# Delta rule and MLP mixer on one core: every step of the recurrence as 64x64 products on compact state, with another order of issue

## The chip, the cores and the metric

The kernel runs on one NeuronCore of one Trainium2 chip. The metric is the device time of one execution in microseconds, the median of several runs. The engines named below are TensorE (PE, with its weight loads as PEld), VectorE (DVE), ScalarE (ACT), GpSimd (POOL) and the queue that issues the DMAs (SP).

## The reference

Two blocks follow each other, all in float32. The first is a delta rule, a recurrence over 768 positions for each of 4 batch elements and 8 heads with 48 features:

```
k_n = k / (norm(k) + 1e-6)
state = 0                                    # (B, H, 48, 48)
for t in range(768):
    y[t]  = q[t] @ state
    v_old = state @ k_n[t]
    state = state + beta[t] * outer(k_n[t], v[t] - v_old)
```

Its output, with the heads side by side, is x of shape (4, 768, 384). The second block is an MLP mixer:

```
u   = x + transpose(relu(transpose(x) @ w_tok1) @ w_tok2)     # along the 768 positions, 256 wide
out = u + relu(u @ w_ch1) @ w_ch2                             # along the 384 channels, 1536 wide
```

## The kernel before

**The recurrence in blocks.** The 768 positions of a batch element are cut into 12 chunks of 64 (C = 64), so there are 48 steps r0 to r47, and r12, r24 and r36 begin a new batch element with an empty state. Within a chunk the recurrence is solved with a 64x64 triangular matrix. `prep` builds the matrices of two chunks from k and q (a unit u), `invert` inverts the triangular blocks of 32 by rows on DVE, `join` puts the two halves together with 32x32 products, and the result lies in the tile `gm`. A step then is a short chain: the state is multiplied with k (and q), v is subtracted, the result is multiplied with the inverse, and that product `w` makes the update of the state and the rest of the output `y`.

**Two forms of a step.** The first element (r0 to r11) runs through `recur_early`. It holds the state of each of the 8 heads once, as 48 rows in one half of the partitions, and makes five groups of 8 products (head by head, 64 rows and 64 columns of the array, 48 columns of moving data): `p_k` (L655), the first part of `p_y` (L665), `p_w` (L676), `p_s` (L684) and the second part of `p_y` (L695). The eight products of a group alternate between two quarters of the array, one in each half of the rows and of the columns. The other three elements (r12 to r47) run through `recur`. It holds two heads at a time as a block-diagonal state twice as wide (`s_bd`, `rw_bd`), half of it zeros, and makes three groups of 4 products of the whole array with 96 columns of moving data: `p_q` (L730) for k and q together, `p_w` (L746) and `p_s` (L756) for state update and output together. Because the halves lie in different places, DVE subtracts in two instructions each (L734, L764) and adds the output in one or two more (L773, L776); ACT copies `w` in two (L749) and `p_q`'s q half in one (L751).

**The mixer.** `mixer(b)` takes the finished element: products `p_1` along the positions (L887) into `p_h` (L900), a transpose, then for pairs of chunks the wide products into 1536 channels (plain at L973 for the first element, a form with seven products in place of eight at L818 for the others) and back (L992). Its weights come in pieces that ACT, DVE and POOL round on their way (`round_weights`, L246 to L266).

**The order of the work.** Nothing is scheduled at run time. Every job is a generator, and a long text called `order` says which job issues its next piece: `r` is a step of the recurrence, `m` the mixer, `p`, `i`, `f`, `h`, `j`, `k`, `v` preparation and inversion, `w` a piece of weights, `s` sums of weights. `x`, `z` and `Y` are products of zeros into `p_warm` (L200, L210), which nobody reads. Each engine works through its own instructions in that order, waiting on semaphores where an operand isn't there. The PSUM pools are `prep` (2 buffers), `seq` (2), `mlp` (3) and one for `p_warm`; before, `p_y` of the early steps takes one of `mlp`, and `p_q`, `p_k`, `p_w` and `p_s` take those of `seq`.

Of the kernel before, what the change touches and what calls it, by code (L numbers as in the profile page):

```python
# [8 lines left out]
FP32 = mybir.dt.float32  # L9
# [14 lines left out]
def kernel(  # L24
# [128 lines left out]
    GW = 2 * C + D  # L153
# [6 lines left out]
    r_bd = w_bd = const.tile([128, NP, 2 * D], FP32, name="rw_bd")  # L160
    s_bd = tiles("s_bd", [128, NP, 2 * D], 2)
# [29 lines left out]
    def place(u):  # L191
        return NV + u if u < 2 else (u - 2) % NV

# [123 lines left out]
    walked = set()  # L317

# [52 lines left out]
    def gm_of(u):  # L371
        return gms[place(u)]

    def prep(u):
# [46 lines left out]
        for p in range(NP):  # L421
            nc.tensor.transpose(p_t[:, p], qp[:, 2 * p : 2 * p + 2], ident)
        turned.add((False, u))
        yield
        nc.scalar.copy(kqt_q, p_t)
        yield
        scaler.tensor_tensor(
            out=blocks(gm)[:, :, :, 2 * C :], in0=kst,
# [12 lines left out]
        for cc in range(2):  # L441
            nc.vector.tensor_tensor(  # L442
                out=blocks(gm)[:, :, cc, 0 : 2 * C].rearrange(
                    "s p (two n) -> s p two n", two=2
                ),
                in0=p_g[cc],
                in1=mb[:, :, cc, None, :].to_broadcast([128, NP, 2, C]), op=ALU.mult,
            )
            yield
# [32 lines left out]
    def quarters(u):  # L482


        rnd, j = round_of[u]
        for i in range(4):
            r = slice(HB * i, HB * i + HB)
            cols = slice(HB * (i % 2), HB * (i % 2) + HB)
            lo = (4 * j + i) * NB
            yield (  # L490
                gm_of(u)[r, :, cols], (r, slice(0, HB), slice(j * NB, j * NB + NB)),
                slice(lo, lo + NB),
            )
# [114 lines left out]
    def join(u):  # L608

        done = joined_16 if u < NCH else inverted  # L610
        wt = gm_of(u)[:, :, 0:C]
# [23 lines left out]
    def recur_early(t):  # L635

        u, cc = divmod(t, 2)
        assert t == len(steps)  # L640
        steps.append(t)
        gm, kqt = gm_of(u), kqts[place(u)]
        if t == 0:
            xbs[0] = mlp_pool.tile([128, NCH, DM], FP32, name="xb", tag="xb")
        y = xbs[0][C * cc : C * cc + C, u].rearrange("s (p n) -> s p n", p=NP)
        s0, s1 = s_bd[t % 2][:, :, 0:D], s_bd[(t + 1) % 2][:, :, 0:D]
        w = w_bd[:, :, D : 2 * D]
        by_head = [(p, i, PAR[i ^ cc]) for p in range(NP) for i in range(2)]

        p_y = ps_mlp([128, NP, D], "p_y")  # L650
        if t > 0:
            p_k = ps_seq([128, NP, D], "p_k")
            for p, i, r in by_head:
                f = FEATS[i]
                nc.tensor.matmul(p_k[r, p], kqt[f, 2 * p + cc, 0], s0[f, p])  # L655
            yield
            assert u in scaled
            rest = r_bd[:, :, 0:D]
            nc.vector.tensor_tensor(
                out=rest, in0=p_k, in1=vsts[u][:, :, cc], op=ALU.subtract  # L660
            )
            yield
            for p, i, r in by_head:
                f = FEATS[i]
                nc.tensor.matmul(  # L665
                    p_y[r, p], kqt[f, 2 * p + cc, 1], s0[f, p],
                    start=(p == 0), stop=False,
                )
            yield

        assert u in scaled and u in joined
        if t == 0:
            rest = vsts[u][:, :, cc]
        p_w = ps_seq([128, NP, D], "p_w")
        for p, i, r in by_head:
            nc.tensor.matmul(p_w[r, p], gm[r, 2 * p + cc, 0:C], rest[r, p])  # L676
        yield
        nc.scalar.copy(w, p_w)
        yield

        if t < NQ - 1:
            p_s = ps_seq([128, NP, D], "p_s")
            for p, i, r in by_head:
                nc.tensor.matmul(p_s[FEATS[i], p], gm[r, 2 * p + cc, 2 * C :], w[r, p])  # L684
            yield
            for f in FEATS:
                if t > 0:
                    nc.vector.tensor_tensor(
                        out=s1[f], in0=s0[f], in1=p_s[f], op=ALU.subtract
                    )  # L690
                else:
                    nc.vector.tensor_copy(out=s1[f], in_=p_s[f])
            yield
        for p, i, r in by_head:
            nc.tensor.matmul(  # L695
                p_y[r, p], gm[r, 2 * p + cc, C : 2 * C], w[r, p],
                start=(t == 0 and p == 0), stop=(p == NP - 1),
            )
        if cc == 1:
            walked.add(u)  # L700
        yield
        for i in range(2):
            nc.scalar.mul(
                y[:, :, D * i : D * i + D], p_y[PAR[i ^ cc]], 1.0 if t else -1.0
            )
        written.add(t)
        if t == NQ - 1:
            for t_ in (w_bd, *s_bd):
                nc.gpsimd.memset(t_, 0.0)
        yield  # L710

    def recur(t):

# [9 lines left out]
        s0, s1 = s_bd[t % 2], s_bd[(t + 1) % 2]  # L723
        lo, hi = PAR
        ends = (slice(0, D), slice(D, 2 * D))

        if c > 0:
            p_q = ps_seq([128, NP, 2 * D], "p_q")
            for p in range(NP):
                nc.tensor.matmul(p_q[:, p], kqt[:, 2 * p + cc], s0[:, p])  # L730
            yield
            for i in range(2):
                r = PAR[i ^ cc]
                nc.vector.tensor_tensor(  # L734
                    out=r_bd[r, :, ends[i ^ cc]], in0=p_q[lo, :, ends[i]],
                    in1=vsts[u][r, :, cc], op=ALU.subtract,
                )
        else:
            for r, e in zip(PAR, ends):
                nc.gpsimd.tensor_copy(out=r_bd[r, :, e], in_=vsts[u][r, :, cc])  # L740
        yield

        assert u in scaled and u in joined
        p_w = ps_seq([128, NP, 2 * D], "p_w")
        for p in range(NP):
            nc.tensor.matmul(p_w[0 : C + 1, p], gm[:, 2 * p + cc, 0 : C + 1], r_bd[:, p])  # L746
        yield
        for r, e in zip(PAR, ends):
            nc.scalar.copy(w_bd[r, :, e], p_w[lo, :, e])  # L749
        if c > 0:  # L750
            nc.scalar.copy(y, p_q[hi])  # L751
        yield

        p_s = ps_seq([128, NP, 2 * D], "p_s")
        for p in range(NP):
            nc.tensor.matmul(p_s[0 : C + D, p], gm[:, 2 * p + cc, C:], w_bd[:, p])  # L756
# [3 lines left out]
        if c < NQ - 1:  # L760
            for i, e in enumerate(ends):
                f, e2 = FEATS[i], ends[i ^ cc]
                if c > 0:
                    nc.vector.tensor_tensor(  # L764
                        out=s1[f, :, e], in0=s0[f, :, e], in1=p_s[C : C + D, :, e2],
                        op=ALU.subtract,
                    )
                else:
                    nc.vector.tensor_copy(out=s1[f, :, e], in_=p_s[C : C + D, :, e2])
        if c == 0:  # L770
            nc.scalar.mul(y, p_s[lo], -1.0)
        elif cc == 0:
            nc.vector.tensor_tensor(out=y, in0=y, in1=p_s[lo], op=ALU.add)  # L773
        else:
            for i, e in enumerate(ends):
                nc.vector.tensor_tensor(  # L776
                    out=y[:, :, e], in0=y[:, :, e], in1=p_s[lo, :, ends[1 - i]],
                    op=ALU.add,
                )
# [266 lines left out]
    for t in range(B * NQ):  # L1046
        jobs[f"r{t}"] = recur(t) if t >= NQ else recur_early(t)
# [17 lines left out]
    w10*5 Y x z k0 b w2 w1 x*4 Y k0*5 p0 w2*3 w1*2 k1 p0 w3 b*2 k2 k1 Y k3 p0 w2  # L1065
    p0*4 x p0*3 k1*4 p1 w3 p0*2 p1 p0 x k2*3 p1*5 k4 k2 k3 Y k4 Y k4 w3 p1*2 k4 k2
    p2 p1*2 k3 p2 v1 v0 p1 k3 p1 k3*2 p2*2 p3*2 p2*5 w3 p3*3 x Y z p0 p1 p2*4 p0 w1
    z p3*5 Y p0*2 k4 p3 k4 p4*2 p3*2 p1*2 p2 x p4 p2*3 z*2 p3*2 v0 v1 w18 p3*2 p4 p1
    p4 i0*2 k5 v0 w1 p4*2 i0*3 w3 i0*3 p4*4 k6*2 k7 i0*2 w18 i0*2 k6*2 x p4 i0*2
    k5*3 k6 k5 k7 w18 k6 k7 Y z k7*2 i0*2 v1 w6 v0 h1 p5 p4*2 w18 h0 w6 p5 w6*2 p6 z  # L1070
    i0 h0 p6 z p5 f1 h1 k8 w6 f0 w18 f0*2 v0 f0 p4 f1*3 k5 w13*2 h2 w13 f2*2 h2 h0*4
    p7 h0 x z w8*2 j0 w8 p5 h1 w13 h1*2 w13 j0*2 p5 z f2*2 h1 w8 p6 j0*2 h1 p7 p5*4
    h2 w8 w11 v1 h2 w11 r0*2 w11 h2*3 z r0 p5*2 w17*2 p6 p4*2 w17 r0 r1 w17 p5*3
    k8*2 z v1 w17 p5*3 p6 r1 h3 j1 i1 r0 w14 w11 h3 w14 r1*2 k9 k8 r1 w11 w14 i1
    j1*2 k9*3 r1*3 w0 k8 x p6*3 f3 p6 f3 p6 p7 j1*2 v2*3 i1 r2*2 z p7 i1 r2 w0 i1*2
    j2 i1 f3*2 r2*5 h3*3 i1 Y w14 h3 r0 h3 r3*2 k9 i1 j2*2 p8 k9 w0 k8 k7 i1 p8 r3
    p6 k10*2 p6*2 r1 r3 w0*2 x r3*3 v2*2 j2*2 w14 r2 k10 p7*2 j3 r4*3 r3 i1 r4 w9 j3
# [93 lines left out]
```

## Time and profile before

| | |
|---|---|
| median of 3 runs | 699.59 us (699.56 to 701.43) |
| span of the profiled execution | 693.3 us, TensorE's granted clock 0.983 on average |
| around it | the page gives the span alone, so the profiled execution's own time is not told apart from it; the median of the runs stands 6.3 us above the span |
| PE busy | 663.1 us (96%), 7904 products |
| DVE busy | 477.4 us (69%), 1263 instructions |
| ACT busy | 279.1 us (40%) |
| POOL busy | 106.0 us (15%) |

A float32 product is two records in the profile, so a group of 8 products counts as x16 and a group of 4 as x8. PE is pipelined: a product's duration holds the time from its issue to its last result, and the time that it takes from the others is read from the distance of starts or from the chain. Numbers in the views are microseconds unless marked ns.

### The profile page before, as it was taken

What the parts mean: (1) busy time and instruction counts of PE and PEld (TensorE: products, weight loads), DVE (VectorE), ACT (ScalarE), POOL (GpSimd) and SP (SyncE); (2) the same over time, 40 slices, a digit from 0 to 9 for tenths busy, and PEclk for the clock granted to TensorE, in tenths of its full rate; (3) what the DMA queues carried; (4) which work ended last, traced back from release to release, by engine and by line L of the source; (5) the groups of instructions that cost most, each with busy time, mean ns of one, the idle gap of its engine ahead of it and who ended that gap; (6) DMA issues with size and microseconds to landing.
All of it is one profiled execution on the core that took longest, in us unless ns stands there. A gap on an engine that the chain in (4) does not pass through costs nothing.

```text
span 693.3 us, 19064 instructions
## 1 busy us (share of the span) xinstructions
PE 663.1 (96%) x7904; PEld 589.5 (85%) x7904; DVE 477.4 (69%) x1263; ACT 279.1 (40%) x659; POOL 106.0 (15%) x130
## 2 busy tenths in 40 slices
PE   8759989899999999999999999999999999999998
PEld 6437766558999998978999999978999997999997
DVE  7999997998889854797676886368854532252433
ACT  7647674436542243123652515124425240132230
POOL 3236254133322021001120101101000000000000
PEclk9959999999999999999999999999999999999999
DMA  9755667544343244214443103110030000000000
GB/s 180 129 134 109 142 141 173 131 114 97 76 106 73 57 81 78 60 40 93 80 76 75 32 22 78 33 35 16 4 74 2 1 24 1 23 2 24 0 25 23
DMA packets 146902, 46.17 MB, mean 67 GB/s; under 512 B 138080, under 2 KB 141280, under 8 KB 146816
## 3 DMA queue, kind: packets, MB, share of 16 engines
q1 hardware_dynamic: 146816, 44.95, 30.1%
q8 instruction: 62, 1.02, 0.6%
q14 instruction: 24, 0.20, 0.1%
HBM read 35.49 MB, written 9.44 MB: 65 GB/s over the span
## 4 chain that ended last, share of the span: by engine, by line
PE 85%; ACT 4%; DVE 4%; DMA 3%; issue 2%; POOL 1%; SPq 0%; ACTq 0%; POOLq 0%; DVEq 0%
PE p_o L992 24%; PE p_r L818 7%; PE p_c L818 7%; PE p_c L973 6%; PE p_d L818 5%; PE p L887 5%; PE p_h L900 5%; PE p_q L730 4%; PE p_s L756 4%; PE p_w L746 4%; PE p_g L436 3%; PE p_warm L200 3%; DMA d<-in_moe_w_ch_dram 2%; PE p_z L619 2%; PE p_x L628 1%
## 5 line engine op out<-in xcount | busy, mean ns | idle before, releaser
L992 PE MATMUL p_o<-wc,r 128*128 128x192 f32 x720 | 126.4, 328 | 0.6 <-ACT u_t L914 0.6
L992 PEld LDWEIGHTS p_o<-wc,r 128*128 128x128 f32 x720 | 116.7, 190 | 2.7 <-ACT u_t L914 1.1
L918 DVE TENSOR_TENSOR xb<-xb,p_o 128x192 f32<-128x192 f32 x84 | 29.5, 351 | 61.1 <-PE p_o L992 60.8
L558 DVE TENSOR_TENSOR x<-x,sub 128x84 f32<-128x84 f32 (+24 forms) x178 | 61.0, 343 | 6.1
L553 DVE TENSOR_TENSOR sub<-x 128x84 f32<-128x84 f32 (+24 forms) x178 | 57.4, 323 | 3.8
L973 PE MATMUL p_c<-u_t,wc 128*128 128x256 f32 x216 | 50.2, 383 | 0.0
L992 PE MATMUL p_o<-wc,s 128*128 128x192 f32 x288 | 50.1, 327 | 0.0
L264 POOL TENSOR_TENSOR w_f<-w_f,d 128x384 uint32<-128x384 uint32 (+1 forms) x34 | 34.0, 1004 | 89.5 <-DVE w_f L257 45.7
L835 DVE TENSOR_TENSOR r<-p_r,r 128x384 f32<-128x384 f32 x36 | 19.9, 552 | 39.3 <-ACT r L864 29.9
L992 PEld LDWEIGHTS p_o<-wc,s 128*128 128x128 f32 x288 | 46.8, 190 | 0.0
L838 ACT ACTIVATE r<-r 128x384 f32<-128x384 f32 x72 | 37.6, 524 | 19.9 <-DVE r L835 17.5
L818 PE MATMUL p_r<-u_t,wc 128*128 128x128 f32 x324 | 45.4, 276 | 0.0
L818 PE MATMUL p_c<-u_t,wc 128*128 128x128 f32 x324 | 45.4, 276 | 0.0
L358 POOL TENSOR_TENSOR v_st<-v_st,nrm 128x384 f32<-128x384 f32 x24 | 20.4, 851 | 162.3 <-DMA v_st<-in_v_dram 112.1
L973 PEld LDWEIGHTS p_c<-u_t,wc 128*128 128x128 f32 x216 | 39.7, 190 | 5.3 <-issue 0.5
L415 POOL TENSOR_TENSOR mb<-mask_c,cs 128x512 f32<-128x512 f32 x20 | 21.2, 1060 | 143.2 <-DVE cs L397 137.2
L749 ACT COPY rw_bd<-p_w 64x192 f32<-64x192 f32 x72 | 22.3, 310 | 48.3 <-PE p_w L746 47.1
L818 PEld LDWEIGHTS p_r<-u_t,wc 128*128 128x128 f32 x324 | 40.7, 192 | 0.4 <-issue 0.3
L818 PEld LDWEIGHTS p_c<-u_t,wc 128*128 128x128 f32 x324 | 40.5, 192 | 0.2 <-issue 0.2
L442 DVE TENSOR_TENSOR gm<-p_g,mb 128x512 f32<-128x512 f32 x44 | 28.9, 683 | 12.5 <-PE p_g L436 12.2
L845 ACT COPY r<-p_c 128x384 f32<-128x384 f32 x18 | 8.6, 478 | 67.8 <-PE p_c L818 55.2
L200 PE MATMUL p_warm<-warm 128*128 128x512 f32 (+1 forms) x76 | 34.6, 569 | 0.4 <-issue 0.4
(185 smaller groups left out, 1308.9 us busy)
## 6 DMA issues: line engine op xcount, KB each, us to landing
d<-in_moe_w_ch_dram SPq DMA_DIRECT2D x24, 384.0 KB, 3.9
v_st<-in_v_dram SPq DMA_DIRECT2D x96, 48.0 KB, 2.7
out_dram<-xb SPq DMA_DIRECT2D x23, 192.0 KB, 1.8
kpad<-in_k_dram SPq DMA_DIRECT2D x18, 192.0 KB, 3.6
qpad<-in_q_dram SPq DMA_DIRECT2D x18, 192.0 KB, 3.6
kst<-in_k_dram SPq DMA_DIRECT2D x64, 48.0 KB, 2.8
n_dram<-gm SPq DMA_DIRECT2D x72, 32.0 KB, 1.9
gm<-w_dram SPq DMA_DIRECT2D x72, 32.0 KB, 2.1
```

The lines of the kernel that those rows point to most:

```text
L200: nc.tensor.matmul(p_warm[:, 0:m], zero, zero[:, None, :].to_broadcast([128, m, 128]))
L264: nc.gpsimd.tensor_tensor(out=f, in0=f, in1=lo, op=ALU.add)
L442: nc.vector.tensor_tensor(out=blocks(gm)[:, :, cc, 0 : 2 * C].rearrange("s p (two n) -> s p two n", two=2), in0=p_g[cc], in1=mb[:, :, cc, ...
L553: nc.vector.tensor_tensor(out=tmp, in0=y[:, :, 0:s, s : s + 1].to_broadcast([n, k, s, w]), in1=y[:, :, s : s + 1, s + 1 : m].to_broadcast( ...
L558: nc.vector.tensor_tensor(out=y[:, :, 0:s, s + 1 : m], in0=y[:, :, 0:s, s + 1 : m], in1=tmp, op=ALU.add,)
L818: nc.tensor.matmul(p[:, i], weight(g * n + i), b_, start=first and i == 0, stop=True, skip_group_check=True,)
L838: nc.scalar.activation(out, out, ACTF.Relu)
L887: nc.tensor.matmul(p_1[dh], piece_of(w1, c, 0)[:, dh * 128 : (dh + 1) * 128], xb[:, c], start=(c == 0), stop=(c == NCH - 1),)
L900: nc.tensor.matmul(p_h, piece_of(w2, j, c * 128)[:, c * 128 : (c + 1) * 128], r1[j], start=(j == 0), stop=(j == NDH - 1),)
L918: nc.vector.tensor_tensor(out=xb[:, c, e], in0=xb[:, c, e], in1=p, op=ALU.add)
L973: nc.tensor.matmul(p_c[:, k], piece_of(wc1, cb, f * 128)[:, f * 128 : (f + 1) * 128], u_t[:, cb], start=(cb == 0), stop=(cb == NCB - 1),)
L992: nc.tensor.matmul(p, a[:, m], wc2[:, m, j], start=(start and m == 0), stop=(m == NM - 1), skip_group_check=True,)
```

## The change

`recur_early` goes, and a new `recur` does all 48 steps in the compact form. The state `s_t`, the difference `rest` and `w_t` are 128x192 each, with nothing in them but the heads. The eight `p_k` products stay a group of their own. The first part of `p_y` and `p_w` are now issued product by product in turn, and so are `p_s` and the second part of `p_y`. `p_y` is written to the other half of the partitions than before, which puts two neighbouring products of different kind on two quarters in the same rows, and the next two on the other rows. `p_y` moves from the pool `mlp` to `seq`. The columns of `gm` change places (key part first, inverse second, masked product last) so that `p_s` can take 64 columns from column 0. DVE subtracts in one instruction of 128x192 for `rest` and one for the state; ACT copies `w` in one and writes `y` in two. Clearing the block-diagonal tiles on POOL (L709) and copying v there (L740) go. The text `order` is a new one throughout; it has 30 products into `p_warm` where there were 82.

```diff
-    GW = 2 * C + D
+    GW = D + 2 * C
+    KC, TC, GC = slice(0, D), slice(D, D + C), slice(D + C, GW)
-    r_bd = w_bd = const.tile([128, NP, 2 * D], FP32, name="rw_bd")
-    s_bd = tiles("s_bd", [128, NP, 2 * D], 2)
+    rest_t = const.tile([128, NP, D], FP32, name="rest")
+    w_t = const.tile([128, NP, D], FP32, name="w_t")
+    s_t = tiles("s_t", [128, NP, D], 2)
...
-    def recur_early(t):
...
     def recur(t):
...
-            p_q = ps_seq([128, NP, 2 * D], "p_q")
-            for p in range(NP):
-                nc.tensor.matmul(p_q[:, p], kqt[:, 2 * p + cc], s0[:, p])
-            yield
-            for i in range(2):
-                r = PAR[i ^ cc]
-                nc.vector.tensor_tensor(
-                    out=r_bd[r, :, ends[i ^ cc]], in0=p_q[lo, :, ends[i]],
-                    in1=vsts[u][r, :, cc], op=ALU.subtract,
...
+        heads = [(p, i, PAR[i ^ cc], PAR[1 - i]) for p in range(NP) for i in range(2)]
+        if c > 0:
+            p_k = ps_seq([128, NP, D], "p_k")
+            for p, i, r, _ in heads:
+                f = FEATS[i]
+                nc.tensor.matmul(p_k[r, p], kqt[f, 2 * p + cc, 0], s0[f, p])
+            yield
+            nc.vector.tensor_tensor(
+                out=rest, in0=p_k, in1=vsts[u][:, :, cc], op=ALU.subtract
+            )
+            yield
...
+        p_y = ps_seq([128, NP, D], "p_y")
+        p_w = ps_seq([128, NP, D], "p_w")
+        for p, i, r, o in heads:
+            if c > 0:
+                f = FEATS[i]
+                nc.tensor.matmul(
+                    p_y[o, p], kqt[f, 2 * p + cc, 1], s0[f, p],
+                    start=(p == 0), stop=False,
+                )
+            nc.tensor.matmul(p_w[r, p], gm[r, 2 * p + cc, TC], rest[r, p])
+        yield
+        nc.scalar.copy(w_t, p_w)
+        yield
+        on = c < NQ - 1
+        if on:
+            p_s = ps_seq([128, NP, D], "p_s")
+        for p, i, r, o in heads:
+            if on:
+                nc.tensor.matmul(p_s[PAR[i], p], gm[r, 2 * p + cc, 0:C], w_t[r, p])
+            nc.tensor.matmul(
+                p_y[o, p], gm[r, 2 * p + cc, GC], w_t[r, p],
+                start=(c == 0 and p == 0), stop=(p == NP - 1),
+            )
+        yield
+        if on:
+            if c > 0:
+                nc.vector.tensor_tensor(out=s1, in0=s0, in1=p_s, op=ALU.subtract)
+            else:
+                nc.vector.tensor_copy(out=s1, in_=p_s)
+            yield
+        for i in range(2):
+            nc.scalar.mul(
+                y[:, :, D * i : D * i + D], p_y[PAR[1 - i]], 1.0 if c else -1.0
+            )
...
-        jobs[f"r{t}"] = recur(t) if t >= NQ else recur_early(t)
+        jobs[f"r{t}"] = recur(t)
...
     order = """
...
```

## The prediction

> **What bounds the kernel now.** I read the page's shares and slices first, then the stretches, then the chain, then single groups on PE.
>
> ```profile
> PE 663.1 (96%) x7904; PEld 589.5 (85%) x7904; DVE 477.4 (69%) x1263; ACT 279.1 (40%) x659; POOL 106.0 (15%) x130
> PE   8759989899999999999999999999999999999998
> DVE  7999997998889854797676886368854532252433
> PEclk9959999999999999999999999999999999999999
> PE 85%; ACT 4%; DVE 4%; DMA 3%; issue 2%; POOL 1%; SPq 0%; ACTq 0%; POOLq 0%; DVEq 0%
> ```
>
> PE is full from the eighth slice on; DVE is full only in the first thirteen.
>
> ```profile
> 0.00:131.00 131.00, 108.37 (x2597) 80.09 (x2598) 115.59 (x316) 85.01 (x208) 50.93 (x65) 0.91 0.69 143
> 131.00:165.00 34.00, 31.18 (x300) 20.43 (x298) 30.58 (x74) 12.54 (x29) 11.61 (x15) 1.00 0.51 123
> 165.00:231.00 66.00, 65.26 (x653) 60.40 (x654) 58.67 (x168) 28.91 (x69) 14.03 (x15) 1.00 0.34 74
> 231.00:450.00 219.00, 219.00 (x2373) 204.93 (x2372) 152.67 (x408) 79.45 (x191) 25.90 (x31) 1.00 0.31 64
> 450.00:694.00 244.00, 239.29 (x1986) 223.69 (x1985) 119.87 (x301) 73.21 (x164) 3.52 (x4) 1.00 0.07 18
> ```
>
> The columns behind the length are busy PE, PEld, DVE, ACT and POOL. There are two parts. Up to 131 us, where the first mixer starts, DVE works 115.6 of 131 us and PE's 108.4 hold 40 us of zeros into `p_warm`: DVE sets the pace. From there on PE does; its waits after 131 us add up to 4 us. So the price of a change is DVE work ahead of the mixer, plus PE time behind it. The span is 693.3 us and the median of the runs 6.3 us more; I add 6.3 to the span.
>
> **PE time of a late step, before.** Busy time counts overlapping tails, so I take the chain's shares: 4.2% for `p_q`, 4.1% for `p_s`, 3.6% for `p_w`, 11.9% of 693.3 or 82.5 us, 2.29 us for each of 36 steps. The p_q group alone shows why: 0.87 us for 8 records, 109 ns each, though 96 columns at the pace of a p_o (162 ns for 192) would be 81. The load of 128 columns of weights sets it.
>
> **PE time of a late step, after.** The early steps show the new shape. With two quarters in use, groups of 16 records follow each other at 0.51 us:
>
> ```profile
> 70.61 0.67 PE L665 MATMUL p_y<-s_bd,wc 48*64 48x48 f32 x16
> 71.12 0.63 PE L676 MATMUL p_w<-rw_bd,wc 64*64 64x48 f32 x16
> ```
>
> Record by record they start in pairs 6 ns apart, a pair every 58.5 ns. No group of before interleaves four quarters at this size, but once two groups overlap by chance:
>
> ```profile
> 64.32 0.23 PE L695 MATMUL p_y<-rw_bd,wc 64*64 64x48 f32 x2
> 64.37 0.23 PE L665 MATMUL p_y<-s_bd,wc 48*64 48x48 f32 x2
> 64.38 0.23 PE L695 MATMUL p_y<-rw_bd,wc 64*64 64x48 f32 x2
> 64.43 0.23 PE L665 MATMUL p_y<-s_bd,wc 48*64 48x48 f32 x2
> 64.44 0.23 PE L695 MATMUL p_y<-rw_bd,wc 64*64 64x48 f32 x2
> ```
>
> Eight records start between 64.32 and 64.44: both pairs keep their 58.5 ns, so four quarters take 14.6 ns a record. I take 58.5 ns a round for all groups (the other end, pairs only, is the first rival). Each of the step's three groups is 8 rounds, 0.47 us; 33 `p_k` and 2 x 36 interleaved groups make 105 x 0.47 = 49.1 us.
>
> **What is paid for it: leaving and entering the whole array.** The late p_g groups show this price.
>
> ```profile
> 176.87 1.03 PE L730 MATMUL p_q<-s_bd,kqt 128*128 128x96 f32 x8
> 177.83 1.10 PE L436 MATMUL p_g<-kqt 64*64 64x128 f32 x32
> 178.86 1.56 PE L973 MATMUL p_c<-u_t,wc 128*128 128x256 f32 x6
> ```
>
> By the starts of single records, the first p_g begins 205 ns after the last p_q (112 is its pace): 93 ns. The first p_c begins 198 ns after the last p_g round (109 is its pace): 89. The second p_c comes 321 ns after the first (216 is its pace), because its weights were not loaded ahead: 105, or 52 to 75 where other shapes follow. From quarters to sixteenths (L676 to L619 at 65.0 us) it is again 90. So 92 ns a boundary, and 85 more for a return to the whole array. An isolated group thus costs 0.47 + 0.27 = 0.74 us, three of them 2.2 us, almost the 2.29 of before: the change pays only if groups stand beside other tiled groups. How often, the order of the built programs tells. From the first p_h on, PE's order falls into 77 stretches of one array shape before and 201 after: 124 more boundaries, 11.4 us; returns to the whole array go from 38 to 75, 3.1 us. Together 14.6 us.
>
> The new order also moves two things. One unit's p_g group falls behind that point (8 rounds of 109 ns, 0.9 us). The join products p_z and p_x stood together in pairs before and overlapped (both in 0.92 us, 0.50 for one alone); apart they add up to 3.1 us. **PE's sum behind the first p_h: 49.1 + 14.6 + 0.9 + 3.1 - 82.5 = -14.8 us.** The same adding up for the whole order of before gives 552.6 us from there, where the trace has 547.7 (145.6 to 693.3), so its error is about 1%.
>
> **A rule against it.** In the trace, both row halves write the one tile `p_k` at once, starts 6 ns apart. The Trainium skill, "TensorEngine Tiling (Array Packing)", Restrictions and Gotchas, says instead that different row tiles cannot use the same PSUM bank at the same time. By that rule each round would be two, 49.1 us more on PE, and the kernel would be slower, near 729. The row disagrees, and I keep the row.
>
> **The first part.** DVE: in r1 to r10 the state's update is one instruction where it was two (L688, 349 ns; the new 128x192 form is like L659, 356 ns), 3.5 us less. Adding up the group means of all DVE instructions that stand ahead of the first p_h in the issue order gives 141.8 us before and 137.2 after; the other 1.1 us is work that the order puts behind. I take 4.6 us. The five groups of an early step become three and 52 products into `p_warm` go, but PE isn't the bound there: nothing for that. What hid them is DVE's 0.88 busy; if the clock suffers, see the second rival. POOL's copies and clears (3.8 us together) lie beside other work. SP's DMAs are the same ones in another order; the loads of before wait little, and I take nothing.
>
> **DVE and ACT later.** A late step costs DVE 2 x 350 + 2 x 357 + about 620 ns before, and 356 + 357 after: 1.3 us less, 48 us in 36 steps. It hides under PE from 231 us on and relieves 165 to 231, where DVE is 89% busy, so DVE will not take over there. ACT goes from 2 x 310 + 474 to 312 + 2 x 324 ns, 0.13 us less.
>
> **The wait that is added.** `p_y` now lives in one of `seq`'s two buffers until ACT has written it out; the next step's first `p_y` product waits for that at the head of PE's queue, with `p_w` and everything behind it. In the recurrence of before such a wait on L703 is 0.9 us in two cases. I take nothing; the upper end is rival three.
>
> **Sum.** 693.3 - 14.8 - 4.6 = 673.9 us span, 680.2 us time. The same sum at other places of the order (first p_c, first p_o, the end of p_o's first seven groups) gives -19 to -24, so the likeliest case covers 672 to 689: the lower end has all of the -24 and joins that still overlap, the upper has half of the PE gain eaten by short waits at 105 group heads.
>
> **Rivals.**
> One: quarters in the same rows do not overlap in the new order, where neighbouring products share their rows. Then an interleaved group is 16 pairs of 58.5 ns: 72 x 0.47 = 33.7 us more, 714 us, slower. For it: every recurrence group of before uses only two quarters, in different rows. Against: p_g's 32 records start four at a time within 20 ns, and the overlap above. It decides from 0.74 us for an interleaved group on (19.4 / 72 = 0.27 more than 0.47).
> Two: the first part does not shorten. With 52 fewer filler products the clock falls more often; from 35 to 52 us it already stands at 0.52, with PE 10.3 us busy, about 5 us lost. No gain in front gives 684.8; one or two such stretches on the path 690 to 695.
> Three: PE waits for ACT's two writes of `y`. All 36 times in full (0.65 us) is 23.3 us, 703.5; half of it is 692. Against it: between two steps lie mixer products of several us in the order.
>
> **How the numbers follow.** Forecast 0.66 (672 to 689); rival two 0.13, nearly all still faster; rival three 0.11, of which 0.05 faster, 0.04 the same and 0.02 slower; rival one 0.07, slower; below 672, 0.03. A change under 0.3%, 2.1 us, can hardly be told from none. That makes 0.86 faster, 0.05 the same, 0.09 slower. The range 671 to 694 leaves out rival one, the upper half of three, and bits of two and of the low end.
>
> **What would show it.** In the changed profile: interleaved groups of 32 records that take 0.47 us by their starts, with boundaries of 0.09; the first p_h some 5 us earlier, near 141; PE's time from there to the end near 533 us (547.7 - 14.8); DVE's busy share down by 45 us. A group of 0.94 us would mean rival one; a clock under 0.9 in more slices of the first part rival two; waits of PE on ACT's `y` rival three. If PE shows idle slices after the first p_h, the sum by PE time is wrong as such.

## The result and the profile after

| | before | after |
|---|---|---|
| median | 699.58 us (699.54 to 701.43) | 692.03 us (688.98 to 694.03, 4 runs) |
| ratio | | 0.988, 95% interval 0.985 to 0.991 |
| profiled execution: span, clock | 693.3 us, 0.983 | 691.0 us (time 692.83), 0.936 |
| first `p_h` | 145.5 us | 154.1 us |
| first `p_h` to the end | 547.8 us | 537.0 us |

The change makes the kernel 7.5 us faster; 19.4 were forecast. In these two profiles the part behind the first `p_h` became 10.8 us shorter and the part ahead of it 8.6 us longer. One execution of a kernel differs from the next by several us, so a profile is one draw: that of before took some 4.5 us less than the median of before, that of after 0.8 more than its own, and that of e13 below 8.6 more. By the medians the front lost nearer 3.3 us (worked out under "The offset"). The page after, of its parts the busy times, three rows of slices and the chain (x counts records, two to a product, here and in the 7904 of before):

```profile
PE 643.6 (93%) x9696; PEld 562.2 (81%) x9696; DVE 428.9 (62%) x1135; ACT 272.7 (39%) x659; POOL 103.1 (15%) x121
PE   7548977689999999999999999999999999999998
DVE  6988677887888853696464985347823332252433
PEclk9757677579999999999999999999999999999999
PE 81%; DVE 7%; DMA 3%; SPq 3%; ACT 3%; issue 2%; POOL 0%; DVEq 0%; ACTq 0%; POOLq 0%
```

DVE's busy time fell by 48.5 us, about the 45 foreseen, and PE is full behind the first `p_h` as before. The third row is new: the granted clock is under 0.9 in slices two to nine, where before only the third was. The stretches say the same:

```profile
0.00:131.00 131.00, 93.31 (x2430) 71.91 (x2430) 101.55 (x291) 82.16 (x201) 47.76 (x62) 0.73 0.64 137
131.00:165.00 34.00, 30.43 (x242) 19.20 (x243) 29.24 (x75) 10.90 (x25) 8.27 (x9) 0.78 0.45 113
165.00:231.00 66.00, 66.00 (x1148) 58.13 (x1148) 56.00 (x149) 30.68 (x75) 18.48 (x19) 1.00 0.43 94
231.00:450.00 219.00, 218.13 (x3338) 197.46 (x3330) 137.80 (x365) 77.98 (x196) 25.27 (x28) 1.00 0.30 63
```

Up to 131 us the clock is 0.73 where it was 0.91, and DVE works 101.6 us where it worked 115.6: it does less and waits more. The waits of DVE up to the first `p_h` (us in total, times, longest), of after:

```profile
DVE s_t L703 <- PE p_y L694: 4.8, 3, 2.5
DVE gm L450 <- PE p_g L443: 3.4, 3, 1.8
DVE w_f L257 <- DMA d<-in_moe_w_ch_dram: 2.6, 2, 2.3
DVE wc L271 <- ACT d L268: 2.5, 1, 2.5
DVE wc L612 <- ACT wc L612: 2.3, 2, 2.0
DVE t L622 <- PE p_z L627: 1.5, 1, 1.5
```

All rows of this view add up to 25.2 us, 10.7 of them for PE. The same view of before adds up to 10.7 us, 1.0 of them for PE; its largest row and its two for PE:

```profile
DVE gm L604 <- ACT gm L604: 3.9, 7, 1.5
DVE rw_bd L659 <- PE p_k L655: 0.5, 1, 0.5
DVE gm L442 <- PE p_g L436: 0.5, 1, 0.5
```

The new groups are issued as the change draws them, `p_y` and `p_w` in turn. PE's timeline of after, record by record (start, duration):

```profile
329.80 0.61 PE L749 MATMUL p_r<-u_t,wc 128*128 128x128 f32 x4
330.34 0.25 PE L677 MATMUL p_y<-s_t,kqt 48*64 48x48 f32 x1
330.35 0.25 PE L681 MATMUL p_w<-rest,gm 64*64 64x48 f32 x1
330.35 0.25 PE L677 MATMUL p_y<-s_t,kqt 48*64 48x48 f32 x1
330.36 0.25 PE L681 MATMUL p_w<-rest,gm 64*64 64x48 f32 x1
330.43 0.22 PE L677 MATMUL p_y<-s_t,kqt 48*64 48x48 f32 x1
...
330.49 0.22 PE L677 MATMUL p_y<-s_t,kqt 48*64 48x48 f32 x1
...
330.80 0.22 PE L681 MATMUL p_w<-rest,gm 64*64 64x48 f32 x1
330.95 0.69 PE L627 MATMUL p_z<-t,gm 32*32 32x32 f32 x32
```

Four records start within 20 ns, the second round 90 ns after the first, each later one 60. From the first start to the last are 0.46 us, and the next group starts 0.15 us behind that.

### The profile page after: what moved, and what is told of

The parts are those of the page before. It is cut to its first block, busy times and chain, and to the rows that moved or that the text cites. A ratio compares the mean times of both kernels' runs of the same rounds, so it can differ in the third digit from the quotient of the medians.

```text
span 691.0 us, 22497 instructions
## 1 busy us (share of the span) xinstructions
PE 643.6 (93%) x9696; PEld 562.2 (81%) x9696; DVE 428.9 (62%) x1135; ACT 272.7 (39%) x659; POOL 103.1 (15%) x121
## 4 chain that ended last, share of the span: by engine, by line
PE 81%; DVE 7%; DMA 3%; SPq 3%; ACT 3%; issue 2%; POOL 0%; DVEq 0%; ACTq 0%; POOLq 0%
PE p_o L923 24%; PE p_r L749 8%; PE p_c L749 7%; PE p_d L749 5%; PE p_c L904 5%; PE p_h L831 5%; PE p L818 4%; PE p_k L660 4%; PE p_y L677 3%; PE p_g L443 3%; PE p_s L693 3%; PE p_z L627 2%; DVE sub L561 2%; PE p_warm L205 2%; PE p_x L636 2%
## 5 line engine op out<-in xcount | busy, mean ns | idle before, releaser
L561 DVE TENSOR_TENSOR sub<-x 128x84 f32<-128x84 f32 (+24 forms) x178 | 60.4, 339 | 8.1 <-DMA x<-n_dram 4.4
L708 ACT ACTIVATE xb<-p_y 64x192 f32<-64x192 f32 x96 | 31.2, 325 | 47.0 <-PE p_y L694 20.4
L769 ACT ACTIVATE r<-r 128x384 f32<-128x384 f32 x72 | 37.5, 523 | 17.2 <-DVE r L766 15.1
L685 ACT COPY w_t<-p_w 128x192 f32<-128x192 f32 x48 | 15.3, 319 | 67.8 <-PE p_w L681 67.3
L450 DVE TENSOR_TENSOR gm<-p_g,mb 128x512 f32<-128x512 f32 x44 | 28.8, 682 | 15.7 <-PE p_g L443 14.8
L818 PE MATMUL p<-xb,w 128*128 128x384 f32 x96 | 36.4, 529 | 0.0
```

The source lines that it names most:

```text
L450: nc.vector.tensor_tensor(out=blocks(gm)[:, :, cc, D:GW].rearrange("s p (two n) -> s p two n", two=2), in0=p_g[cc], in1=mb[:, :, cc, None, ...
L561: nc.vector.tensor_tensor(out=tmp, in0=y[:, :, 0:s, s : s + 1].to_broadcast([n, k, s, w]), in1=y[:, :, s : s + 1, s + 1 : m].to_broadcast( ...
L708: nc.scalar.mul(y[:, :, D * i : D * i + D], p_y[PAR[1 - i]], 1.0 if c else -1.0)
L769: nc.scalar.activation(out, out, ACTF.Relu)
L818: nc.tensor.matmul(p_1[dh], piece_of(w1, c, 0)[:, dh * 128 : (dh + 1) * 128], xb[:, c], start=(c == 0), stop=(c == NCH - 1),)
```

## The experiments

Two theories were held for the lost front, that is, for the time ahead of the first `p_h`. **A**: the clock; with fewer products of zeros PE runs at half clock, its results come late, and DVE waits. **B**: the new order itself makes DVE wait, and zeros put into it take from PE what they give in clock. Two questions went along: how much of the gain behind the first `p_h` is the interleaving, and how much the order. "At half clock" below is the time up to 165 us at a granted clock of 0.5. Outside of these stretches the clock is full, and nearly all of them last a multiple of 3.4 us.

**e1_fill.** 53 more products into `p_warm` in the order of after, 32 of them `z`, where its trace shows PE waiting.

```diff
-    ... p1 p0 w2*3 p1 k3*2 ... x p3 v0*2 p1*3 ... k6 p4 x p5 ...
+    ... p1 z p0 w2*3 p1 k3*2 ... x p3 v0*2 z*3 p1*3 ... k6 z*4 p4 x p5 ...
```

> The changed kernel with 53 more products of zeros into p_warm (32 of 128x512, 21 of 128x128), put in the order ahead of the PE instructions that waited between 5 and 150 us; nothing else differs. Theory A (the first part lost its time to TensorE's clock, which stood at half speed for some 85 us there because PE was busy too little with full-size products): the mean clock rises from 0.936 to 0.96 or more, the first p_h comes at 146 us or earlier instead of 154, and the time falls to 680 to 686 us. Theory B (the new order itself makes DVE wait in the first part, whatever the clock): the clock may rise, the first p_h stays at 152 to 156 us, and the time at 689 to 694. Theory C (TensorE's instruction fetch stalls, three of 1.3 to 3.1 us): the stalls stay, time within 2 us of 692.

Measured: 689.11 us (686.73 to 689.36), ratio 0.985 (0.981 to 0.990). The half-clock time falls from 85.3 to 37.5 us, the first `p_h` comes at 151.1 us, but DVE's waits are the same, 25.9 us. Of the stalls that its theory C names, the longest (3.1 us) is gone; others of 1.7 and 1.2 us stand in its profile.

**e2_before_less.** Before with its zeros thinned evenly from 82 products to 30, as many as after has.

```diff
-    w10*5 Y x z k0 b w2 w1 x*4 Y k0*5 p0 ... k2 k1 Y k3 p0 w2 ...
+    w10*5 Y x z k0 b w2 w1 x k0*5 p0 ... k2 k1 k3 p0 w2 ...
     # and so on: 52 of the 82 products in x, z and Y left out
```

> The kernel before, with its 82 products into p_warm thinned out evenly to 30 (7 of 128x128, 11 of 128x512, 12 of 64x128), the numbers that the changed kernel has; its recurrence and the rest of its order untouched. Theory A (the clock): half-speed stretches grow from 24 us to 50 us or more, the first p_h moves from 145.5 to 150 us or later, time 703 to 710 us. Theory B (the new order is at fault, not the fillers): the first p_h stays within 2 us of 145.5 and the time within 2 us of 699.6.

Measured: 707.53 us (703.81 to 708.53), ratio 1.012 (1.007 to 1.016). Behind the first `p_h` nothing changes (547.8 us); that itself comes at 157.3 instead of 145.5. Half-clock time rises from 23.9 to 88.7 us, and in DVE's waits two rows come up that before hardly had:

```profile
DVE s_bd L688 <- PE p_s L684: 6.0, 5, 2.9
DVE gm L442 <- PE p_g L436: 3.3, 4, 1.4
```

So in the order of before the zeros are no decoration: without 52 of them it loses 8 us, by way of DVE's waits for PE.

**e3_oldorder.** The new recurrence in the order of before, with its 82 products of zeros (a step cut into as many pieces as that order has, and `p_y` of the first element in the pool `mlp`, since that order needs it there).

```diff
-        p_y = ps_seq([128, NP, D], "p_y")
+        p_y = (ps_mlp if t < NQ else ps_seq)([128, NP, D], "p_y")
-    order = (that of after)
+    order = (that of before, one piece of r23 ahead of p17)
```

> The compact recurrence of the changed kernel, issued in the order of before, with its 82 products into p_warm (one step's third piece is moved ahead by one place, and p_y of the first twelve steps stays in the PSUM pool where it was). Adding up PE's work from the first p_h on by the same prices gives 540.9 us (552.6 before, 537.8 for the changed kernel). Theory A (fillers and clock): clock above 0.97, first p_h within 3 us of 145.5, time 686 to 690 us. Theory B (the new order costs the first part its time): also about 145.5, same time, but then e1 shows no gain. Rival D (the compact groups themselves keep the clock low, since they use little of the array): clock 0.93 to 0.96 and first p_h at 150 or later, time 692 to 697 us.

Measured: 697.58 us (692.15 to 704.64), ratio 0.995 (0.991 to 0.9995). The first `p_h` at 151.0, the part behind it 546.7 us: in the old order the compact recurrence gains only 1.1 us behind the first `p_h`. PE's order falls there into 239 stretches of one array shape, where the order of after makes 201 of the same groups. The part behind the first `p_h` is still 5.8 us longer than the expectation's sum, which isn't explained. Rival D came in partly: with the same order and the same zeros the profile has 44.8 us at half clock, and the mean clock of its executions (median 0.968) is below that of before on the same chip (0.976). So the compact groups seem to lower the clock by themselves; no run tests it apart from the rest.

**e4_split.** After, with the two interleaved pairs issued one group after the other.

```diff
         for p, i, r, o in heads:
             if c > 0:
                 nc.tensor.matmul(p_y[o, p], kqt[f, 2 * p + cc, 1], s0[f, p], ...)
+        for p, i, r, o in heads:
             nc.tensor.matmul(p_w[r, p], gm[r, 2 * p + cc, TC], rest[r, p])
...      # p_s and the second part of p_y likewise
```

> The changed kernel with its interleaving undone: all eight p_y products, then all eight p_w; all eight p_s, then all eight p_y. Order, fillers and everything else as changed. If only two quarters work at a time then (58.5 ns a pair), 72 late groups take 0.47 us more each: 33.7 us, about 725 us. If the engine pulls the second group's products ahead, as it did by chance at 64.3 us in the kernel before, a part of that: 0.2 to 0.3 us a group, 706 to 714 us. If interleaving makes no difference, 692.

Measured: 706.49 us (704.76 to 708.19), ratio 1.011 (1.007 to 1.016); 552.7 us behind the first `p_h`, 15.7 more than after, 0.22 us for each of the 72 interleaved groups there, at the lower end of what the expectation allows for groups that overlap in part. Its timeline shows why:

```profile
331.26 0.49 PE L677 MATMUL p_y<-s_t,kqt 48*64 48x48 f32 x10
331.55 0.26 PE L682 MATMUL p_w<-rest,gm 64*64 64x48 f32 x2
331.59 0.23 PE L677 MATMUL p_y<-s_t,kqt 48*64 48x48 f32 x2
331.64 0.23 PE L682 MATMUL p_w<-rest,gm 64*64 64x48 f32 x2
...
331.75 0.46 PE L682 MATMUL p_w<-rest,gm 64*64 64x48 f32 x10
332.14 0.38 PE L751 MATMUL p_r<-u_t,wc 128*128 128x128 f32 x1
```

The two groups overlap only where they meet, and take 0.88 us from the first start to the next work, where the interleaved ones take 0.61. Interleaving is worth more than the whole change.

**e5_fine, e6_nofill, e7_after_again.** Smaller zeros spread finely; next to none; and after itself once more, all on one chip.

```diff
 # e5_fine: 91 more x (128x128), none larger
-    ... p1 p0 w2*3 p1 k3*2 ... x p3 v0*2 p1*3 ... k6 p4 x p5 ...
+    ... p1 x*2 p0 w2*3 p1 k3*2 ... x p3 v0*2 x*4 p1*3 ... k6 x*7 p4 x p5 ...
 # e6_nofill: only the first two x and the first Y (four products) stay
-    ... w1 z*2 b*2 k1 ... p1 z p2*2 k3 ... x p3 v0*2 ...
+    ... w1 b*2 k1 ... p1 p2*2 k3 ... p3 v0*2 ...
```

> After, with 91 more products into p_warm of the small kind only (128x128, 0.22 us each, 20 us in all), spread over the first 150 us: in each stretch of 3.4 us in which the trace of after used less than 0.4 of the array, a few are put where PE waited, one at a time elsewhere. Theory A (the front lost its time to PE at half clock, which runs whenever the share of the array in use is low): half-clock time falls from 85 us to under 30, the first p_h comes before 148, the time is 684 to 687. Theory B (the new order itself makes DVE wait, and what zeros give in clock they take in PE time): half-clock time falls too, but the first p_h stays at 151 or later as with the 53 larger fillers, 688 to 691.

> After, without 27 of its 30 products into p_warm (the first three are left). Theory A: half-clock time grows from 85 us to over 105, the first p_h comes 3 to 6 us later (157 to 160), 695 to 698. Theory B: the zeros stand where PE waits anyway, nothing moves by more than 1 us, 691 to 693. The part behind the first p_h stays at 537 either way.

> After once more, beside the others on their chip: 692 us, ratio 0.989; half-clock time between 70 and 95 us in front if that is a property of the order, anything else if the stretches fall by chance; 537 us behind the first p_h.

Measured: 697.52 us (691.02 to 704.86; ratio 0.998, 0.995 to 1.002), 689.78 (688.50 to 691.69; 0.989, 0.986 to 0.992) and 691.10 (690.08 to 693.94; 0.992, 0.989 to 0.995). (In e6 six of the 30 products stay, since a `Y` is four, not three as the expectation counts.) e7 repeats after: 88.7 us at half clock and the first `p_h` at 154.5, so both come with the order and not with one execution. e6 speaks against theory A: with hardly any zeros and 95.6 us at half clock, the kernel is no slower than after.

**e8_neworder.** The fourth corner: the old recurrence, its pieces joined to the number of the new one's, in the new order.

```diff
-            yield                      # between p_y's first part and p_w
...
+        # p_y's second part right behind p_s, in one piece
-    order = (that of before)
+    order = (that of after)
```

> The recurrence of before (two forms, block-diagonal late steps) in the order of after, its pieces joined so that each step has as many as the new one; 30 products into p_warm. If the 10.8 us behind the first p_h come from the interleaved groups, PE's sum gives 557.6 - 4.9 (the sum's error on before) = 553 us from the first p_h on, and with a front of 154 to 157 us the time is 709 to 712. If the order alone brought them, about 540 and 696.

Measured: 722.65 us (721.05 to 723.52), ratio 1.035 (1.031 to 1.039); the first `p_h` at 153.9, and 567.8 us behind it. That is 15 more than expected; about half of these are waits of PE (the rows of the view add up to 10.1 us there, against 2.6 in before), first of all for DVE's two-part subtraction, and the rest isn't accounted for:

```profile
PE p_w L745 <- DVE rw_bd L733: 4.4, 8, 0.8
```

| first `p_h` / behind it, us | order of before | order of after |
|---|---|---|
| recurrence of before | 145.5 / 547.8 | 153.9 / 567.8 |
| new recurrence | 151.0 / 546.7 | 154.1 / 537.0 |

Neither part of the change gains more than 1.1 us behind the first `p_h` by itself: the gain is that of both together. The fronts of this table come from single executions. Carried to the median runs (as under "The offset"; an estimate), they are near 150.0 and 153.1 us for the recurrence of before, 149.1 and 153.3 for the new one. So the new order makes the front 3 to 4 us later whichever recurrence it carries, and in the old order the new recurrence gains only about 1 us of the 3.5 that its DVE work was put at.

**e9_no_sg.** After with DVE's two main reads of PE's results replaced in the first part.

```diff
-  nc.vector.tensor_tensor(out=s1, in0=s0, in1=p_s, op=ALU.subtract)
+  nc.vector.tensor_tensor(out=s1, in0=s0, in1=p_s if t >= NQ else rest_t, op=ALU.subtract)
-                in0=p_g[cc],
+                in0=p_g[cc] if u > 9 else ident... ,
```

> After, with two of DVE's reads of PE's results taken away in the first part: in the first element the state's update subtracts rest in place of p_s, and for the first ten units the mask is multiplied with the identity in place of p_g, so that part computes something else. All products are still issued. In after DVE waits 8.2 us there before the first p_h. Theory A (the front is lost where DVE waits for PE's results): these waits go and the first p_h comes 6 to 8 us earlier, 146 to 148, the time is 684 to 686. Theory C (PE, at half clock, is itself behind; DVE's wait only moves to the next result that it reads): the waits appear at rest (p_k) and t (p_z), the first p_h stays at 151 to 154, 689 to 692.

Measured: 693.69 us (692.23 to 696.62), ratio 0.993 (0.990 to 0.996), the first `p_h` at 155.3. DVE's waits fell to 19.3 us, and 4.8 of them had moved to `rest` (`p_k`), as theory C of this expectation has it. But the experiment added work. The multiply with two operands from SBUF took longer than with one from PSUM (durations: least, median, largest; first e9, then after):

```profile
L450 DVE TENSOR_TENSOR gm<-ident,mb x16: 678/1168/1510, 22.3 to 116.5; 128x512 f32<-128x512 f32 x16
```

```profile
L450 DVE TENSOR_TENSOR gm<-p_g,mb x16: 673/681/692, 21.3 to 112.4; 128x512 f32<-128x512 f32 x16
```

DVE's busy time up to 150 us rose from 120.0 to 126.0 us, as much as its waits fell, so the run does not tell whether the waits were on the path.

**e10_aimed, e11_steady.** The fillers of e1 and 27 small ones where e1 still fell to half clock; and 60 small ones at an even pace in place of after's own.

```diff
 # e10_aimed: as e1_fill, and one x each 0.8 us from 58 to 84 and 104 to 123 us
 # e11_steady: as e6_nofill, and one x each 0.75 us from 22 to 30 and 48 to 146 us
```

> After with the 53 larger fillers and 27 more products of 128x128 into p_warm, one each 0.8 us from 58 to 84 and from 104 to 123 us, where that kernel still fell to half clock. Theory A: the two stretches at 71.6 and 112.5 us vanish, DVE's waits on PE fall from 8.8 to under 4 us, the first p_h comes before 148.5, the time is 684 to 686. Theory B (zeros take from PE what they give in clock): first p_h at 151 to 154, 689 to 692.

> After with its own 27 fillers replaced by 60 products of 128x128 (0.22 us each, 13 us in all), one each 0.75 us wherever they fall in the order, from 22 to 30 and 48 to 146 us. Theory A: half-clock time falls from 90 to under 45 us, the first p_h comes at 147 or earlier, 683 to 686. Theory B: half-clock time may fall, but the first p_h is at 151 or later, 689 to 693.

Measured: 688.48 us (686.78 to 689.64; ratio 0.985, 0.981 to 0.989) and 690.08 (685.44 to 692.21; 0.987, 0.982 to 0.992). e10 tests theory A best. Its clock is better than that of before, and yet the first `p_h` comes at 153.0 (some 151.8 at its median). First its clock by slices, then its chain of work from 60 to 150 us, then its largest waits of DVE:

```profile
PEclk9969999999999999999999999999999999999999
```

```profile
by line: PE p_warm L205 24.0%; DVE sub L561 8.4%; issue 8.2%; DVE x L566 6.9%; PE p_g L443 6.3%; PE p_k L660 5.9%; PE p_s L693 4.8%; PE p_y L677 3.9%; DVE w_f L262 3.1%; PE p_z L627 2.6%; PE p_x L636 2.6%; PE p_t L412 2.4%; PE p_z L596 2.3%
```

```profile
DVE wc L612 <- ACT wc L612: 4.9, 2, 3.6
DVE gm L450 <- PE p_g L443: 3.7, 5, 1.3
DVE rest L664 <- PE p_k L660: 2.3, 2, 2.1
DVE s_t L703 <- PE p_y L694: 1.9, 3, 1.3
```

Zeros are a quarter of the path there (5.4% in after), and DVE's waits are still 26.6 us. The clock is restored and the front is not, but here the clock was bought with zeros that stand on the path.

**e12_cap5, e13_cap3.** The fillers of e10, with every run of consecutive ones cut to five or three `x`.

```diff
-    ... i0*4 z*5 h0 ...
+    ... i0*4 x*5 h0 ...        # e13_cap3: x*3
```

> The kernel with the aimed fillers, each run of consecutive fillers cut to at most five products of 128x128 (1.1 us; runs of up to five large ones, 4.3 us, stood there): zeros worth 34 us in place of 49. Theory A (the front is lost to half clock; the aimed fillers only overshot): half-clock time stays under 35 us, p_warm's share of the chain from 60 to 150 us falls from 24% to under 15%, the first p_h comes before 149, 683 to 686. Theory B (in this order zeros have no free place: what they give in clock they take on PE): the first p_h stays at 151 to 154, 688 to 692.

> The same with runs cut to at most three products of 128x128 (0.65 us): zeros worth 27 us. Theory A: if the clock still holds (under 45 us at half) the first p_h comes before 148, 682 to 686; if it falls (70 us and more), 153 to 155. Theory B: 151 to 154 whatever the clock does, 688 to 692.

Measured: 691.49 us (688.77 to 695.31; ratio 0.991, 0.988 to 0.995) and 690.42 (686.64 to 699.01; 0.989, 0.986 to 0.993). In the profile of e12 the first `p_h` comes at 150.3 us, with 27.3 us at half clock; the median run is 2.7 us longer than that one. Zeros still hold 19% of its chain from 60 to 150 us, where theory A asked for under 15%. The one profile of e13 (699.01 us) is not compared.

The front in one table. "Zeros" is the busy time on `p_warm` up to 143 us; DVE's waits are summed over the view's rows up to the first `p_h`. "At the median" is an estimate: median less 1.8 us less the profile's time behind the first `p_h`.

| kernel | zeros, us | at half clock, us | DVE waits: all / for PE, us | first `p_h`, us | at the median, us | median, us |
|---|---|---|---|---|---|---|
| before | 40.6 | 23.9 | 10.7 / 1.0 | 145.5 | 150.0 | 699.6 |
| e2, before with less | 22.8 | 88.7 | 21.6 / 11.5 | 157.3 | 157.9 | 707.5 |
| e6 | 2.3 | 95.6 | 24.4 / 10.7 | 151.2 | 151.8 | 689.8 |
| after | 22.8 | 85.3 | 25.2 / 10.7 | 154.1 | 153.3 | 692.0 |
| e11 | 35.8 | 71.7 | 25.1 / 12.9 | 152.6 | 152.5 | 690.1 |
| e12 | 51.9 | 27.3 | 23.9 / 8.1 | 150.3 | 153.0 | 691.5 |
| e1 | 59.8 | 37.5 | 25.9 / 9.4 | 151.1 | 151.2 | 689.1 |
| e10 | 64.3 | 17.1 | 26.6 / 9.1 | 153.0 | 151.8 | 688.5 |

In the order of before, zeros buy clock and clock buys time. In the new order, from 2 to 64 us of zeros, the waits stay at 24 to 27 us and the first `p_h` within 4 us, or within 2.1 at the medians: e6 with 95.6 us at half clock and e10 with 17.1 both stand near 151.8. (e5, with 51.5 us of zeros, falls out: 161.5 us, its waits 34.6. Its finely spread fillers were worse than hardly any; why was not followed.)

## Why the prediction was wrong

**The step that failed** is the last of the first part: the 52 products fewer and the early groups were put at nothing, since "PE isn't the bound there" and "what hid them is DVE's 0.88 busy". The work term was right: DVE's busy time ahead of the first `p_h` went from 129.0 to 123.7 us, 5.3 less, where 4.6 were forecast. But I took DVE's idle time as given. It went from 16.5 to 30.4 us, 13.9 more; less the 0.7 us by which the work fell further than forecast, that is the way from the forecast 140.9 (145.5 - 4.6) to the measured 154.1. Some 5.3 of these 13.2 us are the draw of the two profiles; by the medians the term is off by 7.9: 4.6 less was forecast, 3.3 more came. A share of 0.88 with hardly any waits for PE was the work of an order, and the change replaced that order "throughout". Nor is it the order alone: in the old one, with all 82 products, the new recurrence brings about 1 us of the 3.5 that its work was put at (e3). So some 2 to 3 of the 7.9 are lost with the recurrence, by the clock, as rival D has it, or otherwise; that stays open. The rest goes with the order. A sum of busy times says nothing of the waits that a new order brings, and the issue order of the changed program, which I used for PE, could have been followed for what DVE waits for as well.

**Rival two** named the right place, and its lower clock came in: 85.3 us at half clock instead of 23.9. The measured 692.03 lies in its band of 690 to 695, which had a chance of 0.13; that it also lies in the stated range of 671 to 694 is no merit of the main sum, and rival three's "half of it", 692, fits by luck. As a cause it is shown for the order of before (e2). For the new order it is only half of an answer. For it: of one kernel's executions those with the higher clock tend to be the shorter ones (before 695.64 us at 0.985 and 703.12 at 0.967; e12 688.77 at 0.978 and 694.92 at 0.968), and single waits follow the clock: DVE's `s_t` at 103 us in after waits 1.2 us where PE is at half clock (after, e7) and 0.1 where it is not (e1). The first of these is a correlation: a run that is late for another reason leaves PE idle and could lose clock by that. Against it: no kernel with the clock restored got its front back to that of before, let alone to the forecast; e1 comes nearest, 151.2 against 150.0 at the medians, and e6 with almost no zeros is as early as e10. What stays open is what the new order would take at full clock if that cost PE nothing; every way I had to raise the clock puts zeros into PE's queue.

**The part behind the first `p_h`.** Forecast 14.8 us less, measured 10.8. The eight other profiles of the interleaved recurrence in the new order (e1, e5 to e7, e9 to e12) have 534.7 to 536.7 us there, so 11.1 to 13.1. The mechanism was right and one term too small. A group was put at 0.47 us and a boundary of 0.09; measured are 0.46 to the last start and 0.15 from there to the next group, 0.05 more. Nearly all groups that a product of another shape follows are like this one. Times 105 groups this is 5 us, enough for the miss of 4. The same adding up for the whole order of after gave 537.8 (expectation of e3) where 537.0 were measured; for before it was 4.9 too high, so an error common to both sums would account for the 5 us not showing in the second. The reason for the 0.46 is also not the one I gave: eight rounds have seven distances, 0.41 us at 58.5 ns, but the first of them is 0.09. The pair of before that I read (63.998 and 64.091 us) shows this already.

**Rivals one and three.** Four quarters overlap at every interleaved group, so rival one is out; e4 gives the price of taking the interleaving away, 0.22 us a group, where this rival had put 0.47, and that kernel is slower than before. Rival three is out: behind 154 us after's waits of PE show none on ACT's writes of `y`; the largest is 1.3 us of "issue".

**The rule against the change** (The Trainium skill, "TensorEngine Tiling (Array Packing)", Restrictions and Gotchas) put the time near 729; the row that I kept held: in after the two row halves of one `p_k` start 6 or 7 ns apart, those of one `p_w`, with products of `p_y` between them, 14 ns, and each lasts over 200 ns.

**The offset.** I added 6.3 us to the span. The true distance is 1.8 us (692.83 to 691.0 in after; also 691.01 to 689.2 in e7 and 689.64 to 687.8 in e10). So the profiled execution of before took about 695.1 us, and I put the other 4.5 us to the front. That is an assumption, since no run shows where the median run spends them; the nine profiles of one back above lie within 2.3 us. With 547.8 us behind it, the median run of before then has its first `p_h` near 150.0, and that of after near 153.3. Between the medians the front lost 3.3 us and the back gained 10.8, which is the 7.5 that the runs show. Of the 11.9 us by which the forecast missed, 7.9 are the front and 4.0 the back.

## What to carry to other kernels

When an order of issue is replaced as a whole, the busy times of the old profile give the work and not the waits: the waits have to be worked out anew, and "not the bound" holds only for the order that made it so. Small products on quarters of the array paid here only where quarters of both halves were interleaved product by product and the order gave them neighbours; behind the first `p_h` each part alone lost time or gained 1.1 us. Zeros that hold the clock up are worth what the order leaves free on PE: 52 of them were worth 8 us in one order, and 53 at most 2 to 3 in the other, where the intervals of the two ratios overlap (e1 and after). All versions with other fillers lie within some 4 us of after, e5 behind it; the fastest, e10, stands at 688.5 us (interval of its ratio 0.981 to 0.989) beside after's 691 to 692 (0.985 to 0.991 and 0.989 to 0.995).

## What the runs showed of the hardware

**A busy PE can fall to half clock and stay there.** One stretch of after (columns as above):

```profile
64.20:81.30 17.10, 16.25 (x348) 12.95 (x349) 11.28 (x38) 8.72 (x22) 4.98 (x6) 0.50 0.50 105
```

PE is busy for 95% of it and gets half its clock throughout; in the 3.4 us ahead of it, at full clock, it was busy for 76%. The Trainium skill, "TensorE: Matmul & The Clock Gate", Part 1, says that the clock follows how busy PE has been in windows of 3.4 us. The lengths of the stretches agree with the window (3.4, 10.2, 17.1, 20.5 us); for small products "busy" does not. If each record is weighted with the share of the array that it covers and 0.84 ns a column (from a `p_o`, 162 ns for 192), the six windows of after ahead of a fall hold 0.08 to 0.28 of the array, and those that stayed at full clock 0.28 and more. That is an estimate from records, and no run here tests it by itself. In other kernels the line is not as sharp: by the same weighting a window of 0.30 fell in e1, and three of 0.19 to 0.22 stayed up in before.

**Four quarters in turn take 14.6 ns a record**, as four records in a round of 58.5 ns; the round behind a change of shape takes some 90.

**DVE reading two operands from SBUF** took 678 to 1510 ns for the multiply that takes 673 to 692 with one of them in PSUM (e9). The Trainium skill, "SBUF — State Buffer", SBUF: two separate sides, has a rule for this: a DVE instruction with two SBUF inputs and a GpSimd one that reads SBUF exclude each other. The trace agrees: the five short ones (678 to 684 ns) start with no GpSimd instruction running, the eleven long ones all start while one runs, and ten of these end 0.55 us after it has ended.

**A stall without a cause in the profile.** PE stopped in the middle of one group, with nothing that the view names:

```profile
98.71 0.71 PE L596 MATMUL p_z<-r,gm 32*32 32x16 f32 x34 [3.14 <-issue]
```

The same program in e7 stops there for 2.2 us. The queue of instructions moved 76 packets in after and 62 in before; that the one comes from the other was not tried.
